# Eight units' products in plain float32, paired loads and two weight queues in an attention and MLP kernel

## The chip, the cores and the metric

The kernel runs on one core of one Trainium2 chip. A core has TensorE (PE, with its weight loads shown as PEld), VectorE (DVE), ScalarE (ACT), GpSimd (POOL) and SyncE (SP), and its DMAs share 16 DMA engines. The metric is the device time of the run in microseconds, lower is better.

## The reference

Attention with a window of 32 keys to either side and 32 global tokens, then an MLP on its output, all with float32 results. Eight batches, eight heads, 512 local and 32 global tokens, heads of 64:

```python
s_ll = np.where(np.abs(pos[:, None] - pos[None, :]) <= 32, scale * (q_l @ k_l.T), -1e9)
s_l = np.concatenate([scale * (q_l @ k_g.T), s_ll], axis=-1)
out_l = softmax(s_l) @ np.concatenate([v_g, v_l])          # local queries
out_g = softmax(scale * (q_g @ [k_g, k_l].T)) @ [v_g, v_l]  # global queries
x = concat([out_g, out_l]).transpose(0, 2, 1, 3).reshape(B * S, 512)   # 8 * 544 rows
h = x @ w_in                  # 512 x 2048
g = 0.5 * h * (1 + erf(h / sqrt(2)))
out = g @ w_out               # 2048 x 512
```

(shortened; the transposes of single heads are left out). The two weight matrices arrive as 64-bit floats, everything else as 32-bit.

## The kernel before, in words

**Units and keys.** Attention is cut into 64 *units*: batch, half of the local tokens (256 queries), pair of heads. The MLP is cut into 17 *keys*: one for each batch and half (256 rows, fed by four units) and one, "g", for the 256 rows of all global queries, which comes last. A key runs over 16 slices f of the 2048 hidden columns: `h` (12 matmuls of 128x256, L667 to L669), gelu on two slices at once (`gf`), its split (`gh`, `gl`) and `acc` (6 matmuls of 128x512, L696 to L698, three for each of two tiles of 128 rows). `ob` (L150) copies the two `acc` tiles out of PSUM, and SP stores them (L711, L715).

**Split products.** TensorE multiplies in a rounded form of float32 (fp32r in the rows). To keep float32 accuracy every operand is split: a copy in fp32r (high part) and the difference to it (low part, the subtractions of L157), and a product is the sum of three matmuls: high by high, low by high, high by low. So q becomes `q1` and `q2`, k `k1` and `k2`, v the tile `vs`, the transposed softmax `at`, the MLP's input `xh` and `xl`, and each weight `wi` and `wo` two halves of 512 columns.

**A unit.** SP loads k, q and v (`kn`, `qn`, `vr`; L330, L337, L281 to L292). For the first eight units (`NPE`) TensorE transposes k and q into PSUM (`kp` L344, `qp` L351); for later ones DVE does. Then come the splits; `s` (12 matmuls, L408: two windows, three terms, two heads); the masking with the maximum (L427); exp on ACT (L306); the normalisation (L457 to L461 on DVE, `ge` L468 and L473 on POOL or DVE); the transposes of the softmax (`t`, L482 to L485); `at` and its low part (L150, L496); `o` (8 matmuls, L512, whose output holds high and low terms side by side, 128 partitions by 256), which a copy on ACT (L517) and two additions on DVE (L522, L523) gather in `xs`; and `sg` (2 matmuls, L536), the scores of the global queries, which are collected in `sgr`. `xh` and `xl` are then made from `xs`.

**Weights.** 32 chunks of 512 KB, loaded by DMAs that ACT issues (`wraw`, L176 and L180), become float32 in five steps: `w1` (ACT L193), `w2` (ACT L197), `w3` (shift and or, DVE L201), `w4` (the high part, DVE or ACT, L152 or L150) and `w5` (the low part, L157 on POOL or DVE). The raw chunks live in two pools of three and four buffers; the memory of the pool of four is used by MLP tiles once its chunks are done.

**What sets the order.** A planner in Python (`step`, L721 on) builds a list of steps with the engine or engines that may run them, a modelled duration (`DUR`), what they need, which buffers they take and free, and a due time: the key's number times 60, less a lead for attention (`AHEAD`), plus a number for each kind of step (`OFF`, and `OFF0` too for the units and steps of the first two keys). It then plays the program: again and again it takes the step that could start first, and among those the one due first. The order that comes out is forced on each engine's queue, so an instruction that waits holds back all behind it on its engine. `EARLY` and `LATER` name the engines that may run a step.

Of the kernel before, what the change touches and what calls it, by code (L numbers as in the profile page):

```python
# [35 lines left out]
NB = 10  # L36
# [11 lines left out]
    "gmin": 0.8, "gex": 0.8, "gn": 0.55, "gt": 0.57, "gah": 0.5, "gal": 0.6, "gagh": 0.25, "gagl": 0.2,  # L48
# [9 lines left out]
AHEAD = 23.2  # L58
# [3 lines left out]
EARLY = {"gh": "a", "gl": "p", "gvc": "va", "gvl": "p", "k1": "va", "nf": "p", "ns": "pv", "q1": "va", "vc": "va", "vl": "p", "xh": "v", "xl": "vp"}  # L62
LATER = {"gh": "va", "gl": "p", "gvc": "va", "k1": "va", "ns": "p", "q1": "va", "vc": "va", "vl": "p", "w4": "va", "w5": "pv", "xh": "va", "xl": "vp"}

OFF = {
    "ah": -0.7, "al": 6.9, "b": -2.3, "c": -29.8, "e": -41.0, "g": -10.7, "gagh": 1.8,
    "gagl": -54.7, "gah": 6.3, "gal": -15.7, "gex": 14.0, "gh": 11.7, "gl": 9.5, "glv": 2.5,
    "gmin": -27.2, "gn": 11.1, "go": -11.0, "gsh": 1.1, "gsl": -36.6, "gt": 0.5, "gvc": -40.0,
# [3 lines left out]
    "sga": -6.9, "sgc": -6.1, "t": 0.4, "tg": 10.0, "tgh": -5.3, "tgl": -5.0, "tk": -0.4,  # L72
    "tq": 90.4, "vc": -12.0, "vl": -51.1, "vm": -24.8, "w1": 46.7, "w2": -27.2, "w3": -0.3,
    "w4": 1.1, "w5": 11.8, "wl": 5.5, "x": 14.9, "xh": -18.0, "xl": -0.4,
}
OFF0 = {
    "ah": -0.8, "al": -7.0, "b": -3.9, "c": -2.0, "e": 2.1, "g": -14.9, "gagh": -6.6, "gagl": -22.2,
    "gah": -2.9, "gal": -27.8, "gex": 11.7, "gh": 2.1, "gl": 2.6, "glv": -16.8, "gmin": -1.6,
    "gn": -44.0, "go": 9.5, "gsh": -16.7, "gsl": -15.1, "gt": 2.8, "gvc": 26.0, "gvl": -7.5,
# [6 lines left out]
}  # L86
NPE = 8
UNP = 100
WB = 10
# [3 lines left out]
def attn_mlp(ctx, tc, q_l, k_l, v_l, q_g, k_g, v_g, w_in, w_out, out):  # L93
# [178 lines left out]
    def load_v(e, u):  # L272
# [15 lines left out]
        for r0, src, s0, n in ef:  # L288
            nc.sync.dma_start(out=raw[r0:r0 + n, 4:6, :], in_=src[s0:s0 + n])
# [738 lines left out]
```

## Time and profile before

| | |
|---|---|
| median of 3 runs | 1084.24 us (1084.11 to 1084.83) |
| the profiled execution, its own time | 1083.86 us |
| its span in the trace | 1082.1 us |
| TensorE busy | 1026.0 us, 95% of the span, 7064 matmuls |
| DVE, ACT, POOL busy | 693.6, 695.1, 453.6 us |
| mean granted TensorE clock | 0.985 of full speed |
| loads and stores | 71.34 MB, 66 GB/s on average |
| chain that ended last | PE 89%, DMA 4%, DVE 4%, SP 1%, ACT 1% |

TensorE is the engine that is nearly always busy; the shares are means over the whole span, so a stage with another limit is hidden in them. Times of single instructions are in microseconds from the span's start. A busy time of an engine is the union of its instructions; neighbouring ones overlap a little, so the sum over groups of instructions is larger.

### The profile page before, as it was taken

To read this page: it belongs to the slowest core of one execution; us is meant where nothing else is said; L and a number is where in the kernel's file an instruction comes from. 1 tells how busy PE (TensorE), PEld (TensorE's weight loads), DVE (VectorE), ACT (ScalarE), POOL (GpSimd) and SP (SyncE) were. 2 spreads that over 40 slices of the span, in tenths; PEclk is the share of its full clock that TensorE was granted. 3 is DMA by queue.
4 is the path that set the end of the run, shared out by engine and by line. 5 is a ranking of instruction groups with operands and counts; after the bars stand their busy time and mean duration, and the time that the engine had idled before them with its cause. 6 is when DMAs were issued, how large, how long until landed. Compare 5 with 4: busy or idle time off the path is not lost.

```text
span 1082.1 us, 21840 instructions
## 1 busy us (share of the span) xinstructions
PE 1026.0 (95%) x7064; PEld 916.6 (85%) x7064; DVE 693.6 (64%) x2089; ACT 695.1 (64%) x1634; POOL 453.6 (42%) x548
## 2 busy tenths in 40 slices
PE   3759789999999999999999999999999999999997
PEld 2549578999999899998999988988899889999896
DVE  4777876768677776667666776667675776642000
ACT  4766766767686776657866676657864876663221
POOL 4444234534444454344434444334444544343121
PEclk9969979999999999999999999999999999999999
DMA  6455623323322322222322233222222223110000
GB/s 171 127 149 170 182 62 73 62 56 61 75 49 60 66 58 63 37 70 42 69 53 64 44 68 61 50 57 54 68 42 69 42 65 59 44 34 21 1 20 20
DMA packets 274738, 71.34 MB, mean 66 GB/s; under 512 B 260032, under 2 KB 268224, under 8 KB 274624
## 3 DMA queue, kind: packets, MB, share of 16 engines
q1 hardware_dynamic: 263872, 53.17, 23.4%
q10 hardware_dynamic: 10752, 16.78, 5.1%
q8 instruction: 56, 0.92, 0.4%
q14 instruction: 58, 0.48, 0.2%
HBM read 60.95 MB, written 8.91 MB: 65 GB/s over the span
## 4 chain that ended last, share of the span: by engine, by line
PE 89%; DMA 4%; DVE 4%; SPq 1%; ACT 1%; issue 1%; POOL 0%; ACTq 0%; DVEq 0%; POOLq 0%
PE h L667 12%; PE h L669 12%; PE h L668 12%; PE acc L696 11%; PE acc L698 11%; PE acc L697 11%; PE o L512 6%; PE s L408 5%; PE t L482 2%; PE go L622 2%; DMA kn<-in_k_l_dram 2%; PE sg L536 1%; PE t L483 1%; DMA vr<-in_v_l_dram 1%; PE gt L581 1%; DMA wraw<-in_moe_w_out_dram 1%
## 5 line engine op out<-in xcount | busy, mean ns | idle before, releaser
L667 PE MATMUL h<-xh,wi 128*128 128x256 f32 x1088 | 313.9, 289 | 11.3 <-POOL ge L468 6.1
L669 PE MATMUL h<-xh,wi 128*128 128x256 f32 x1088 | 305.8, 281 | 1.1 <-POOL wi L157 1.1
L668 PE MATMUL h<-xl,wi 128*128 128x256 f32 x1088 | 305.6, 281 | 0.1
L157 POOL TENSOR_TENSOR gl<-gf,gh 128x512 fp32r<-128x512 f32 x136 | 176.1, 1295 | 267.4 <-ACT gh L150 166.0
L667 PEld LDWEIGHTS h<-xh,wi 128*128 128x128 f32 x1088 | 206.4, 190 | 22.3 <-POOL ge L468 6.4
L696 PE MATMUL acc<-wo,gh 128*128 128x512 f32 x544 | 220.0, 404 | 1.7 <-DVE wo L152 1.7
L698 PE MATMUL acc<-wo,gh 128*128 128x512 f32 x544 | 215.1, 395 | 0.0
L697 PE MATMUL acc<-wo,gl 128*128 128x512 f32 x544 | 214.8, 395 | 0.0
L668 PEld LDWEIGHTS h<-xl,wi 128*128 128x128 f32 x1088 | 206.7, 190 | 6.6 <-DVE xl L157 0.4
L669 PEld LDWEIGHTS h<-xh,wi 128*128 128x128 f32 x1088 | 206.4, 190 | 1.3 <-POOL wi L157 1.3
L306 ACT ACTIVATE gf<-h 128x512 f32<-128x512 f32 x136 | 81.4, 598 | 103.0 <-PE h L669 88.8
L157 POOL TENSOR_TENSOR vs<-vr,vs 128x512 fp32r<-128x512 f32 x64 | 83.3, 1302 | 107.5 <-DVE vs L152 57.0
L698 PEld LDWEIGHTS acc<-wo,gh 128*128 128x128 f32 x544 | 102.0, 188 | 25.3 <-DVE wo L157 0.4
L306 ACT ACT_TABLE_LOAD x87 | 111.6, 1283 | 9.9 <-PE h L669 8.7
L696 PEld LDWEIGHTS acc<-wo,gh 128*128 128x128 f32 x544 | 102.2, 188 | 18.1 <-issue 1.9
L468 POOL TENSOR_TENSOR ge<-a_t,sm 128x256 f32<-128x256 f32 x64 | 60.2, 941 | 135.8 <-DVE sm L458 75.8
L306 ACT ACTIVATE a_t<-a_t,sm 128x192 f32<-128x192 f32 (+1 forms) x256 | 116.6, 457 | 0.5
L697 PEld LDWEIGHTS acc<-wo,gl 128*128 128x128 f32 x544 | 102.3, 188 | 13.5
L427 DVE CUSTOM_DVE_ANT_0 a_t<-s,mask 128x192 f32<-128x192 f32 (+1 forms) x256 | 80.9, 369 | 48.1 <-PE s L408 47.8
L496 DVE TENSOR_TENSOR at<-t,at 128x512 fp32r<-128x512 f32 (+1 forms) x128 | 75.6, 618 | 41.9 <-ACT at L150 41.4
L150 ACT ACTIVATE gh<-gf 128x512 fp32r<-128x512 f32 x98 | 61.8, 631 | 49.5 <-PE acc L698 48.4
L512 PE MATMUL o<-at,vs 128*128 128x256 f32 x512 | 80.1, 294 | 7.7 <-DVE at L496 7.7
(111 smaller groups left out, 1660.8 us busy)
## 6 DMA issues: line engine op xcount, KB each, us to landing
wraw<-in_moe_w_in_dram ACTq DMA_DIRECT2D x16, 512.0 KB, 4.3
wraw<-in_moe_w_out_dram ACTq DMA_DIRECT2D x16, 512.0 KB, 3.9
vr<-in_v_l_dram SPq DMA_DIRECT2D x128, 64.0 KB, 2.1
gvr<-in_v_l_dram SPq DMA_DIRECT2D x64, 128.0 KB, 2.5
out_dram<-ob SPq DMA_DIRECT2D x32, 256.0 KB, 2.1
kraw<-in_k_l_dram SPq DMA_DIRECT2D x224, 36.0 KB, 2.0
qraw<-in_q_l_dram SPq DMA_DIRECT2D x224, 32.0 KB, 1.9
vr<-in_v_l_dram SPq DMA_DIRECT2D x64, 32.0 KB, 2.2
```

The lines of the kernel that those rows point to most:

```text
L150: nc.scalar.activation(out=out, in_=in_, func=AF.Copy)
L157: (nc.vector if e == "v" else nc.gpsimd).tensor_sub(**kw)
L306: nc.scalar.activation(func=func, **kw)
L427: nc.vector.tensor_tensor_reduce(out=a_t[:, j, aoff[half][i]:aoff[half][i] + w], in0=s[:, c:c + w], in1=masks[half][:, c:c + w], scale=1.0 ...
L496: nc.vector.tensor_sub(out=at[:, 1], in0=st.pop((u, "t", j))[:, :n * P].rearrange("p (n q) -> p n q", q=P), in1=at.bitcast(F32)[:, 0])
L512: nc.tensor.matmul(out=o[:, :, qsl], lhsT=l.rearrange("p s e -> p (s e)"), rhs=r, start=(n == 0), stop=(n == 3), skip_group_check=True)
L667: nc.tensor.matmul(out=h, lhsT=hi, rhs=xh, start=(c == 0), stop=False, skip_group_check=True)
L668: nc.tensor.matmul(out=h, lhsT=hi, rhs=xl, start=False, stop=False, skip_group_check=True)
L669: nc.tensor.matmul(out=h, lhsT=lo, rhs=xh, start=False, stop=(c == NCC - 1), skip_group_check=True)
L696: nc.tensor.matmul(out=acc[t], lhsT=gh[:, f % 2, tsl], rhs=hi, start=(f == 0), stop=False)
L697: nc.tensor.matmul(out=acc[t], lhsT=gl[:, f % 2, tsl], rhs=hi, start=False, stop=False)
L698: nc.tensor.matmul(out=acc[t], lhsT=gh[:, f % 2, tsl], rhs=lo, start=False, stop=(f == NF - 1))
```

## The change

The first eight units (keys (0, 0) and (0, 1)) multiply in plain float32, with no low parts: `st_k0` and `st_q0` copy k and q out of PSUM, `s` is 4 matmuls instead of 12 and `sg` 1 instead of 2, `st_a0` copies the transposed softmax once, `st_o0` makes 8 matmuls of 64x128 out of v as it was loaded, and `st_c0` copies the result to `xs` in two instructions. Their k, q and v are loaded for two units at once into tiles (`raws`, `vr`) that are set up once; k of the global tokens isn't loaded a second time for batch 0. Loads of weights may be issued by SP as well as ACT (`WLE`), as the planner finds. The first four slices of `h` of key (0, 0) go to the PSUM banks of `acc` and one quarter after the other, as their part of `xh` is there (`HQ`). For the last two slices of key "g" the twelve `acc` matmuls are ordered by tile, `ob` of the second tile may run on either engine, its last `gl` runs on DVE, and ACT issues two of the eight stores. Nearly all numbers of `OFF`, `OFF0`, some of `DUR` and the engines in `EARLY` and `LATER` are new; `ALAP` and `DELTA` are switched off.

```diff
-AHEAD = 23.2
+AHEAD = 7.41
...
-    "ah": -0.7, "al": 6.9, "b": -2.3, "c": -29.8, "e": -41.0, "g": -10.7, "gagh": 1.8,
+    "ah": 3.1, "al": -21.0, "b": -70.1, "c": -34.1, "e": -32.8, "g": -12.4, "gagh": 7.5,
...
+WLE = "as"
...
+HQ = 4
 NPE = 8
 UNP = 100
-WB = 10
+WB = 14
...
-            nc.scalar.dma_start(
+            (nc.sync if e == "s" else nc.scalar).dma_start(
...
-    def load_v(e, u):
+    def load_v(e, u, n=1):
...
+        raw = vr[:, :, i0:i0 + n].rearrange("p s i j e -> p s (i j) e")
+        vh, gh = v_l[b, 2 * p:2 * p + 2 * n].rearrange("h s e -> s h e"), v_g[b, 2 * p:2 * p + 2 * n].rearrange("h s e -> s h e")
...
+        kl, kg = k_l[b, 2 * p:2 * p + 4].rearrange("h s e -> s h e"), k_g[b, 2 * p:2 * p + 4].rearrange("h s e -> s h e")
...
+    def st_q0(e, u):
+        t = ap_.tile([P, CH], F32, name="qt", tag="qt")
+        copy(e, t, st[u, "qt"])
+        st[u, "qt"] = t
...
+        prods = [(st[u, "qt"], st[u, "kt"])] if (u, "kt") in st else [(q1, k1), (q2, k1), (q1, k2)]
         for i, (k0, w, qt) in enumerate(windows(half)):
-            for n, (qq, kk) in enumerate(((q1, k1), (q2, k1), (q1, k2))):
+            for n, (qq, kk) in enumerate(prods):
...
+    def st_a0(e, u, j):
+        n = 4 if j == 0 else 3
+        at = ap_.tile([P, n, P], F32, name=f"ao{j}", tag=f"at{j}")
+        st[u, "at", j] = at
+        copy(e, at, st.pop((u, "t", j))[:, :n * P].rearrange("p (n q) -> p n q", q=P))
...
+    def st_o0(e, u):
...
+        for n, (slot, qsl) in enumerate(((ts_, qs), (tf, qf), (2, qf), (3, qs))):
+            for j in range(2):
+                a = at0 if n == 3 else (at0, at1)[j]
+                nc.tensor.matmul(out=o[0:64, j, qsl], lhsT=vr[:, slot, u[2] % 2, j, :], rhs=a[:, n, :],
+                                 start=(n == 0 and j == 0), stop=(n == 3), skip_group_check=True)
+
+    def st_c0(e, u):
+        o = st.pop((u, "o", 0))
+        for j in range(2):
+            copy(e, xs[64 * j:64 * j + 64, u[2]], o[0:64, j])
...
+            if key == (0, 0) and f < HQ:
+
+                st["h", key, f // 2] = ps_o.tile([P, 2, CH], F32, name="h", tag=f"acc{f // 2}")
...
-        for t in range(2):
+
+        last = key == "g" and f >= NF - 2
+        for t, f in ([(f - NF + 2, x) for x in (NF - 2, NF - 1)] if last else [(t, f) for t in range(2)]):
...
-                nc.sync.dma_start(out=out[r0:r0 + SG, :], in_=o[32 * n:32 * n + 32, :])
+                (nc.sync if t == 0 or n % 2 == 0 else nc.scalar).dma_start(out=out[r0:r0 + SG, :], in_=o[32 * n:32 * n + 32])
...
-            step(("gl", key, f), ml_gl, (key, f), "p", d + 1.3, [("gh", key, f)], [("gl", (key, f))], [("gf", (key, f))], early=not n)
+            step(("gl", key, f), ml_gl, (key, f), "v" if key == "g" and f == NF // 2 - 1 else "p", d + 1.3, [("gh", key, f)], [("gl", (key, f))], [("gf", (key, f))], early=not n)
```

On TensorE, what stands right before the first h product of the program is, in the kernel before, `s` of a unit with its three terms and `sg` with two (`k_141` and `q_143` are the high parts, `k_142` and `q_144` the low ones):

```order
L408 MATMUL s<-k_141,q_143 128x192 x2
L408 MATMUL s<-k_141,q_144 128x192 x2
L408 MATMUL s<-k_142,q_143 128x192 x2
L408 MATMUL s<-k_141,q_143 128x224 x2
L408 MATMUL s<-k_141,q_144 128x224 x2
L408 MATMUL s<-k_142,q_143 128x224 x2
L536 MATMUL sg<-k_141,gs 128x256
L536 MATMUL sg<-k_142,gs 128x256
L667 MATMUL h<-xh,wi 128x256
```

and in the changed kernel, at the same place:

```order
L439 MATMUL s<-kt,qt 128x192 x2
L439 MATMUL s<-kt,qt 128x224 x2
L369 MATMUL qp<-ident,raws 128x128 x2
L361 MATMUL kp<-ident,raws 128x128 x2
L363 MATMUL kp<-ident,raws 128x64
L592 MATMUL sg<-kt,gs 128x256
L726 MATMUL h<-xh,wi 128x256
```

`s` went from 12 to 4 matmuls and `sg` from 2 to 1, and the transposes of the next unit's q and k (`qp`, `kp`) moved in between.

On SP, the loads of k and v of one of the first eight units are, in the kernel before:

```order
L330 DMA kn<-in_k_l_dram 128x2x64
L330 DMA kn<-in_k_l_dram 32x2x64
L330 DMA kn<-in_k_g_dram 32x2x64
L330 DMA kn<-in_k_l_dram 64x2x64 x2
L281 DMA vr<-in_v_l_dram 128x2x64 x2
L289 DMA vr<-in_v_l_dram 32x2x64
L289 DMA vr<-in_v_g_dram 32x2x64
L289 DMA vr<-in_v_l_dram 64x2x64
L292 DMA vr<-in_v_g_dram 32x64 x2
L292 DMA vr<-in_v_l_dram 32x64 x2
```

and in the changed one, where a load brings two units and loads of weights stand between them:

```order
L354 DMA raws<-in_q_l_dram 128x4x64 x2
L186 DMA wraw<-in_moe_w_out_dram 128x1024
L345 DMA raws<-in_k_l_dram 128x4x64
L345 DMA raws<-in_k_l_dram 32x4x64
L345 DMA raws<-in_k_g_dram 32x4x64
L345 DMA raws<-in_k_l_dram 64x4x64
L348 DMA raws<-in_k_l_dram 64x2x64 x2
L182 DMA wraw<-in_moe_w_in_dram 128x4x256
L295 DMA vr<-in_v_l_dram 128x4x64 x2
L303 DMA vr<-in_v_l_dram 32x4x64
L303 DMA vr<-in_v_g_dram 32x4x64
L303 DMA vr<-in_v_l_dram 64x4x64
```

Each load has four heads where it had two, and the weights' loads moved from ACT's queue in between them.

On TensorE, at the end of the program, the last h product of key "g" and what follows it, in the kernel before (36 `acc` matmuls follow in all, to the end in this alternation of the two tiles):

```order
L669 MATMUL h<-xh,wi 128x256
L696 MATMUL acc_14031<-wo,gh 128x512
L697 MATMUL acc_14031<-wo,gl 128x512
L698 MATMUL acc_14031<-wo,gh 128x512
L696 MATMUL acc_14032<-wo,gh 128x512
L697 MATMUL acc_14032<-wo,gl 128x512
L698 MATMUL acc_14032<-wo,gh 128x512
```

and in the changed kernel (12 follow in all; the five left out here are of the second tile):

```order
L728 MATMUL h<-xh,wi 128x256
L757 MATMUL acc_13548<-wo,gh 128x512
L758 MATMUL acc_13548<-wo,gl 128x512
L759 MATMUL acc_13548<-wo,gh 128x512
L757 MATMUL acc_13548<-wo,gh 128x512
L758 MATMUL acc_13548<-wo,gl 128x512
L759 MATMUL acc_13548<-wo,gh 128x512
L757 MATMUL acc_13549<-wo,gh 128x512
```

The last h moved 24 matmuls towards the end, and the tiles no longer alternate.

## Rows read from the trace of the kernel before

**Rows 1.** Busy time by stretch: window, length, busy of five engines, PEclk, DMA share, GB/s.
```profile
0.00:77.20 77.20, 40.94 (x181) 29.41 (x181) 51.36 (x152) 47.62 (x114) 35.85 (x64) 0.91 0.58 155
77.20:150.50 73.30, 60.95 (x386) 52.97 (x386) 61.13 (x152) 55.03 (x117) 26.12 (x29) 0.92 0.52 145
...
500.00:600.00 100.00, 99.61 (x714) 89.77 (x712) 68.71 (x214) 67.11 (x160) 43.41 (x55) 1.00 0.28 59
10.00:20.00 10.00, 6.08 (x30) 4.20 (x31) 6.37 (x22) 5.42 (x16) 1.59 (x3) 1.00 0.68 192
110.00:120.00 10.00, 8.24 (x56) 6.83 (x54) 7.98 (x21) 6.58 (x12) 2.60 (x2) 1.00 0.75 219
```

**Rows 2.** Timeline of PE: start, us, instruction; in brackets idle before and releaser.
```profile
77.19 0.55 PE L667 MATMUL h<-xh,wi 128*128 128x256 f32 x1 [6.14 <-POOL ge L468]
...
150.47 0.58 PE L667 MATMUL h<-xh,wi 128*128 128x256 f32 x1 [3.89 <-DVE xh L152]
```

**Rows 3.** Chain of waits from 0 to 78 us: shares by line, then pieces (start, us).
```profile
by line: DMA kn<-in_k_l_dram 22.0%; DMA vr<-in_v_l_dram 11.6%; DMA wraw<-in_moe_w_out_dram 9.9%; SPq L330 9.1%; DMA qn<-in_q_l_dram 5.8%; issue 4.5%; PE o L512 4.0%; SPq L281 3.6%; DMA vr<-in_v_g_dram 3.4%; PE kp L344 3.0%; PE s L408 1.9%; 
...
1.75 5.37 DMA kn<-in_k_l_dram
...
31.64 0.43 PE t L482 x2
```

**Rows 4.** Chain of waits around 300 us: pieces on PE (start, us).
```profile
297.77 0.22 PE t L482 x2
...
298.53 0.12 PE h L667
...
299.94 0.86 PE s L408 x12
300.80 1.15 PE o L512 x8
301.95 0.23 PE acc L696
...
303.35 0.26 PE sg L536 x2
```

**Rows 5.** DVE by line and shape, 77.2 to 150.5 us: busy, mean ns, idle before.
```profile
L157 DVE TENSOR_TENSOR wo<-wraw,wo 128x512 fp32r<-128x512 f32 x7 | 4.8, 687 | 0.1
...
L522 DVE TENSOR_TENSOR xs<-o,xs 64x256 f32<-64x256 f32 x8 | 3.3, 414 | 0.5 <-ACT xs L517 0.3
```

**Rows 6.** DVE by line, 0 to 77.2 us.
```profile
L201 DVE SCALAR_TENSOR_TENSOR wraw<-wraw 128x512 int32<-128x512 int32 x12 | 8.4, 702 | 7.9 <-ACT wraw L197 7.9
L427 DVE CUSTOM_DVE_ANT_0 a_t<-s,mask 128x192 f32<-128x192 f32 (+1 forms) x24 | 7.6, 369 | 0.2 <-PE s L408 0.2
L496 DVE TENSOR_TENSOR at<-t,at 128x512 fp32r<-128x512 f32 (+1 forms) x8 | 4.9, 622 | 2.5 <-ACT at L150 2.4
L461 DVE TENSOR_TENSOR a_t<-a_t,sm 128x512 f32<-128x512 f32 x5 | 4.4, 870 | 0.2
...
L152 DVE CAST wi<-wraw 128x512 fp32r<-128x512 f32 x3 | 1.3, 423 | 0.1
...
L559 DVE TENSOR_SCALAR gsm<-gsm 128x1 f32<-128x1 f32 x1 | 0.2, 153 | 0.0
```

**Rows 7.** DMA issues: count, KB each, median us from issue to landing.
```profile
wraw<-in_moe_w_in_dram ACTq DMA_DIRECT2D x16, 512.0 KB, 4.3
...
out_dram<-ob SPq DMA_DIRECT2D x8, 64.0 KB, 1.7
```

**Rows 8.** Timeline of the end, ACT and SP.
```profile
1067.81 0.60 ACT L306 ACTIVATE gf<-h 128x512 f32<-128x512 f32 x1 [2.19 <-PE h L669]
1070.61 0.63 ACT L150 ACTIVATE gh<-gf 128x512 fp32r<-128x512 f32 x1 [2.20 <-PE acc L698]
...
1075.45 1.30 ACT L150 ACTIVATE ob<-acc 128x512 f32<-128x512 f32 x2 [4.21 <-PE acc L698]
...
1076.07 3.63 SPq L711 DMA_DIRECT2D out_dram<-ob  x8
```

More of the change, by code (lines that the diff above doesn't have):

```diff
@@ L666, in ml_hc @@
         hi, lo = wi[:, f, c * P:c * P + P], wi[:, f, 512 + c * P:512 + c * P + P]
-        nc.tensor.matmul(out=h, lhsT=hi, rhs=xh, start=(c == 0), stop=False, skip_group_check=True)
+        nc.tensor.matmul(out=h, lhsT=hi, rhs=xh, start=(c == 0 and not (key == (0, 0) and f < HQ and f % 2)), stop=False, skip_group_check=True)
         nc.tensor.matmul(out=h, lhsT=hi, rhs=xl, start=False, stop=False, skip_group_check=True)
@@ L798, in attn_mlp @@
         g = (b, p // 2) if half else None
-        bx = [("b", x) for x in both] + ([("gmin", g)] if g else [])
+        bx = [("b", x) for x in both] + ([("gmin", g)] if g and GX else [])
         for j in range(2):
@@ L810, in attn_mlp @@
-        step(("al", u, 1), st_al, (u, 1), "v", f0 - 3.4, [("ah", u, 1)], [], [("t", (u, 1))], dur="al1")
-        step(("lv", u), load_v, (u,), "s", f0 - 18.0, [("o", units[n - 2], 1)] if n > 1 else [], [("vr", u)], issues=9, size=0.25, after=pu and ("lv", pu))
-        step(("vm", u), st_vm, (u,), "p", f0 - 8.0, [("lv", u)])
-        step(("vc", u), st_vc, (u,), "va", f0 - 6.0, [("vm", u)], [("vs", u)], early=n < 8)
-        step(("vl", u), st_vl, (u,), "p", f0 - 4.5, [("vc", u)], [], [("vr", u)], early=n < 8)
@@ new lines, in attn_mlp @@
+        if n < NPE and not odd:
+            step(("lv", u), load_v, (u, 2), "s", f0 - 18.0, [], [("vr0", u), ("vr1", units[n + 1])], issues=9, size=0.5, after=("lv", units[n - 2]) if n else None)
+            step(("vm", u), st_vm, (u, 2), "p", f0 - 8.0, [("lv", u)])
+        elif n >= NPE:
+            step(("lv", u), load_v, (u,), "s", f0 - 18.0, [("o", units[n - 2], 1)], [("vr%d" % odd, u)], issues=9, size=0.25, after=("lv", pu if n > NPE else units[n - 2]))
+            step(("vm", u), st_vm, (u,), "p", f0 - 8.0, [("lv", u)])
@@ L855, in attn_mlp @@
             w = [("w5", 2 * f)] if not n else []
-            if f in (0, NF - 1):
+            if not n and f < HQ:
+                for c in range(NCC):
+                    step(("hc", key, f, c), ml_hc, (key, f, c), "t", C0 + W * f + 0.1 * c,
+                         w + [("hc", key, f, c - 1) if c else ("hc", key, f - 1, 0) if f else None, ("xl", key, c)],
+                         [("acc", "h")] if not f and not c else [], [("xx%d" % c, key)])
+            elif f in (0, NF - 1):
                 for c in range(NCC):
@@ L862, in attn_mlp @@
             else:
-                step(("h", key, f), ml_h, (key, f), "t", C0 + W * f, w + [("h", key, f - 1) if f > 1 else ("hc", key, 0, NCC - 1)],
+                step(("h", key, f), ml_h, (key, f), "t", C0 + W * f,
+                     w + ([("hc", key, x, NCC - 1) for x in range(HQ)] if not n and f == HQ else [("h", key, f - 1) if f > 1 else ("hc", key, 0, NCC - 1)]),
                      hb, [("xx%d" % c, key) for c in range(NCC)])
@@ L869, in attn_mlp @@
             d = C0 + W * (2 * f + 2)
-            step(("g", key, f), ml_g, (key, f), "a", d, [("h", key, 2 * f + 1) if 2 * f + 1 < NF - 1 else ("hc", key, NF - 1, NCC - 1)], [("gf", (key, f))], [("h", (key, f))], table="gelu")
+            step(("g", key, f), ml_g, (key, f), "a", d, [("hc", key, x, NCC - 1) for x in (2 * f, 2 * f + 1)] if not n and 2 * f < HQ else [("h", key, 2 * f + 1) if 2 * f + 1 < NF - 1 else ("hc", key, NF - 1, NCC - 1)], [("gf", (key, f))], [("h", (key, f)) if n or 2 * f >= HQ else ("acc", "h")], table="gelu")
@@ new lines, in attn_mlp @@
+    if ALAP:
+        todo, after = {}, {}
+        for x in nodes.values():
+            todo[x["name"]] = 0
+        for x in nodes.values():
+            for y in x["needs"]:
+                todo[y] += 1
+        stack = [x for x in nodes.values() if not todo[x["name"]]]
+        while stack:
+            x = stack.pop()
+            nm = x["name"]
+            kind = nm[0]
+            if nm in after and kind not in ("h", "hc", "mo") and not (kind[0] == "g" and kind not in ("g", "gh", "gl")):
+                x["due"] = after[nm] - min(x["eng"].values()) + OFF.get(kind, 0.0)
+            for y in x["needs"]:
+                after[y] = min(after.get(y, 1e9), x["due"] - 0.3)
+                todo[y] -= 1
+                if not todo[y]:
+                    stack.append(nodes[y])
@@ L940, in attn_mlp @@
                         due += 100.0
-                c = (t, due, ENG.index(k), x, k)
-                if best is None or c[:3] < best[:3]:
-                    best = c
-        assert best, "no step can start"
+                can.append((t, due, ENG.index(k), x, k))
+        assert can, "no step can start"
+        first = min(can, key=lambda c: c[:3])
+        best = min((c for c in can if c[4] == first[4] and c[0] <= first[0] + DELTA.get(first[4], 0.0)), key=lambda c: (c[1], c[0]))
         t, due, _, x, k = best
```

220 lines of the change are left out of this document (129 added, 91 removed), and 27 rows, old and new, of tables (DUR, OFF, OFF0).

## The prediction

> **What bounds the kernel now.** I read the busy time by stage first, then the chain of waits of the start, then single instructions. The stages [rows 1] show a TensorE that is full from some 160 us on (99.61 of 100 us busy in the stretch from 500 us) and whose unit and MLP work there is not touched by the change. What can move lies at the two ends. Up to 77.2 us TensorE is busy 40.9 us, in short pieces; there the first four units go through attention and no product of the MLP runs. At 77.19 us the first h product starts, after 6.14 us of idle [rows 2]. From there to 150.5 us it is busy 61.0 of 73.3 us. At 150.47 us the last quarter of the second key's first h product starts, after 3.89 us of idle behind an xh [rows 2]; from then on there is always work. I call 0 to 77.2 us stage one, 77.2 to 150.5 us stage two and their end the handover.
>
> In the instruction order of the changed kernel the handover is the same place: the products of units 0 to 7 are done, 201 of the h matmuls stand before it in both, and 72 of acc where it was 78. What follows it is the same work to within those 6 matmuls (1.4 us). So the time is: the profiled 1083.86 us, less what the handover moves forward, and what the tail changes. The profiled execution is 0.4 us under the median of the runs.
>
> The chain of waits of stage one [rows 3] names the reason for its length: loads of k 22.0%, of v 11.6% and 3.4%, of q 5.8% and of weights 9.9% are 52.7% of 78 us, 41 us of landing time, in ten pieces one behind the other, the first of 5.4 us, and SP's own issuing is 12.7% more (10 us). Neither DVE (51.4 of 77.2 us) nor ACT (47.6) is full [rows 1].
>
> **The change part by part.** *Loads by pairs.* Of units 0 to 7 two share one set of loads: some 17 DMAs in place of 31, with the same bytes. On the chain I count six landings where ten stood (k of pairs 0, 1 and 2, v of pairs 0 and 1, one weight), and half of SP's issuing: 41 x 4/10 + 5 = 21 us less, the first h at 56 us. What is late next is DVE or the bytes. DVE: counted along the changed order up to the last xl before the first h, at the means of [rows 5, 6]: 14 shift-ors at 0.70 us, 10 casts at 0.42 and 7 subtractions at 0.69 of weights, 22 score reductions at 0.37, four normalisations of 0.87, ten copies out of PSUM at the cast's 0.42, and some 10 us of smaller ones: 44 us. Neighbours overlap: the 27 groups of stage one before add to 57 us, of which [rows 6] shows the largest and the last, where the union is 51.4, so 44 becomes 40 us. At DVE's present share (51.4 of 77.2) that is 60 us. Bytes: up to the first h the kernel moves 155 GB/s x 77.2 us = 12.0 MB [rows 1], and the changed one wants the same by its own first h (16 weight loads of 0.52 MB each, four pairs of k and q, two to three of v). At the 192 GB/s that the stretch from 10 to 20 us reached [rows 1] these are 62.5 us, at the 219 of the stretch from 110 us 55, at today's mean 77. I take the first h at 63 us, since the bytes are the latest of the three; ends 55 and 77.
>
> *Weights on two queues.* Each of 32 loads may now be issued from SP or ACT; SP takes 26 of them in the order. A load of w_in lands 4.3 us after its issue [rows 7] and would from either, so the gain is only that ACT's instructions no longer stand behind an issue that waits for a buffer. I price that at nothing (below nothing is the second rival). The Trainium skill, "DMA: Bandwidth & Descriptors", section "Issuing engines are not separate DMA queues", says that DMAs from different engines run on the same 16 DMA engines, and that a second issuing engine saves only sequencer time. By that the second queue brings no bytes per second, which is the first rival; the price of nothing agrees with it.
>
> *Plain float32 products, units 0 to 7.* DVE and POOL lose the low halves. Stage two on DVE, from [rows 5] and their like: sixteen xs additions (8 of them 3.3 us, their twins as much) become four copies, 5.0 less; eight low halves of at (4.9 us, as in stage one [rows 6]) become five copies of 0.6 like ACT's [rows 8], 1.9 less; nine casts and low halves of k, q and vs at some 0.42 [rows 6], 3.8 less; against that 18 weight subtractions in place of 13 (POOL gives them up), 3.4 more, two casts (0.8), normalisations, reductions and ge that the planner puts there, 2.0 more. 61.1 becomes 56.6 us, which at the present share of 83% is 68 us. TensorE pays: in a full stretch s of a unit takes 0.86, o 1.15 and sg 0.26 us [rows 4]. No plain float32 product is in the trace. The nearest rows are float32 transposes: two of 128 columns in 0.22 us at full clock, in 0.43 us at the start [rows 3], so 0.11 to 0.21 us per 128 columns. For s (4 of 208 columns), sg (288) and o (8 of 128) that is 1.8 to 3.7 us a unit, against 2.3 now: from 0.4 less to 1.4 more. I take 1.4, since a product of two full operands is hardly cheaper than moving one. Units 0 to 3 lie in stage one, where TensorE idles 36 us. Units 4 to 7 cost 5.6 us in stage two, whose 12.4 us of idle cover it; TensorE needs 61 + 5.6 = 66.6 us there, and 5.6 us would be the price if the cover were gone. The Trainium skill, "FP8 and Floating Point Precision", section "TensorE Precision Notes", gives true float32 four passes. At four times the 0.12 us of a split product of 256 columns [rows 4] that is an estimate of 4.0 us a unit, 1.7 more than today, 6.8 us in stage two, still under its idle time.
>
> So stage two wants 68 us of DVE at its share and 66.6 of TensorE, in place of 73.3. Two engines that full wait for each other; I take 71, ends 64 and 78. The handover is at 63 + 71 = 134 in place of 150.5: 16.5 us earlier.
>
> *The tail.* Today both acc tiles end within 0.7 us, ACT copies both in 1.30 us and SP issues eight stores in 3.63 us, the last landing 1.7 us after its issue [rows 7, 8]. The last twelve products are now ordered by tile, so the first tile ends six products of 0.23 us [rows 4], 1.4 us, before the last one, 0.7 earlier than now, and its four stores go out beside the second tile's products. ACT takes two stores of the second tile. The last issue starts some 1.6 us earlier; nothing hides that. But the order also moves the last h. Before, 36 products of acc follow it (8.4 us), and the first 24 cover the last gelu, gh and gl. Now twelve follow, all of them of that last pair, so TensorE waits: gelu 0.60 and gh 0.63 [rows 8], gl now on DVE 0.69 [rows 5], four handovers of 0.1 (gelu starts 0.1 after the last h [rows 8]), 2.3 us, of which one product that needs gh alone fills 0.2. That is 2.0 us of idle that is not there today. The tail is 0.4 us longer; ends 1.6 less, if the wait is hidden after all, and 1.0 more.
>
> *The planner.* All due times, the lead of attention over the MLP (23.2 to 7.41) and some durations are new, so every key after the handover has a new order with the same work. At [rows 1]'s 0.39 us of idle per 100 us there is nothing to win. I price it at nothing; it can only lose (third rival).
>
> Sum: 1083.86 - 16.5 + 0.4 = 1067.8, with the 0.4 to the median 1068 us.
>
> **The rivals.** First, the bytes: loads stay at 155 GB/s as in stage one now, the first h stays at 77, stage two takes 71, handover 148: 1083.86 - 2.3 + 0.4, or 1082 us. For it: the same bytes, on the same 16 engines. Against: the DMA share there is 0.58, and 0.75 at 219 GB/s [rows 1].
>
> Second, slower: unit loads stuck behind weights on SP. In the new order loads of q, k (twice) and v stand behind weight loads that must wait until an older chunk's buffer is converted: load 4.3 [rows 7], ACT 2 x 0.6 as its copies take [rows 8], DVE 0.70 + 0.42 [rows 6] and 0.69 [rows 5], some 7 us a turn. At four places before the first h that is up to 28 us: 1096 us. It turns the result from 4 us a place on (16.1 us over four). Against: the buffers are seven there, and in today's start SP waits little for weights. The opposite, that these waits replace waits of ACT, is in my sum.
>
> Third, the new order stalls after the handover: one more DVE step of 0.7 us [rows 5] ahead of the first h at each of 15 key changes is 10.5 us, 1078 us. For it: attention runs 16 us closer to its use, and in the order the h of a new key is cut into quarters between o's. Against: nothing but TensorE is full there.
>
> That the change doesn't do what it says I leave out: the built order has four s matmuls where twelve stood, and the paired loads.
>
> **How the numbers follow.** Forecast, 1058 to 1075 us: 0.61. Still earlier handover (55 + 64 = 119, 31.5 earlier): 0.07, down to 1053. First rival 0.12, third 0.09, second 0.11. The range from 1056 to 1081 holds the forecast, half of the early case, most of the third rival and of the first what comes out a little under its 1082. 0.2% is 2.2 us, about what a measurement can tell from no change, so same is 1082.1 to 1086.4. Faster 0.82 (forecast, early case, third, half of the first), same 0.07 (the rest of the first, a little of the second), slower 0.11.
>
> **What would show it.** The first h near 63 us and the handover near 134. The chain up to there with k and v landings in about six pieces; DMA near 190 GB/s in stage one; DVE about 40 and 57 us busy in the two stages. Plain s and o at about 0.2 us per 128 columns. If the first h comes at 75 or later with DMA under 165 GB/s, the first rival holds; if SP waits for w5 of a chunk ahead of a unit's loads and TensorE for those, the second; if TensorE idles over 5 us after 160 us, the third. The tail: 2 us of idle on TensorE behind the last h, and from the last product to the end 1.6 us less.

## The result, and the profile after

The changed kernel takes 1068.62 us (median of 4 runs, 1066.75 to 1069.45) where the kernel before takes 1084.53: a ratio of 0.9851, with a 95% interval of 0.9834 to 0.9868. The prediction was 1068 us. The total came out, but two of its steps did not, and they cancel: that it came so close is luck.

The profiled execution took 1066.75 us, its span is 1064.9 us. The marks that cut the span into stages, with the prediction and with a second profiled execution (1068.59 us):

| us | before | predicted | after | after, again |
|---|---|---|---|---|
| first h | 77.2 | 63 | 56.9 | 57.3 |
| handover (last quarter of the second key's first h) | 150.5 | 134 | 125.9 | 129.5 |
| from there to the end of the last product | 925.6 | 927.6 | 933.0 | 932.4 |
| from there to the end of the span | 6.0 | 4.4 | 6.0 | 4.9 |

The handover comes 24.5 us earlier (21.0 in the second execution) where 16.5 were forecast; of these, 7.4 (6.8) are given back between the handover and the last product, where 2.0 were forecast.

Busy time by stretch of the changed kernel (window, length, busy of PE, PEld, DVE, ACT, POOL, PEclk, DMA share, GB/s); the first two stretches answer to the first two of [rows 1], and the third is the rest up to the last product:

```profile
0.00:56.90 56.90, 37.35 (x188) 25.10 (x189) 38.62 (x118) 40.02 (x98) 18.41 (x40) 0.97 0.75 215
56.90:125.90 69.00, 61.62 (x421) 53.66 (x420) 61.99 (x152) 52.89 (x119) 15.64 (x17) 1.00 0.53 146
125.90:1058.90 933.00, 925.82 (x6489) 831.69 (x6487) 547.36 (x1764) 603.77 (x1432) 380.88 (x434) 1.00 0.25 52
20.00:30.00 10.00, 9.57 (x36) 6.73 (x37) 6.85 (x23) 9.47 (x28) 5.40 (x6) 1.00 1.05 343
```

The kernel before from its handover to its last product, and stage two in the second execution of the changed kernel:

```profile
150.50:1076.10 925.60, 924.08 (x6499) 834.26 (x6499) 581.08 (x1788) 591.80 (x1404) 391.60 (x456) 1.00 0.25 52
```

```profile
57.30:129.50 72.20, 66.23 (x421) 58.01 (x420) 63.25 (x154) 52.75 (x119) 15.86 (x18) 0.92 0.53 140
```

To be seen there: stage one moves 215 GB/s where it moved 155, and 343 in its best ten microseconds. DVE is busy 38.6 of 56.9 us (40 were forecast), then 62.0 of 69.0 (56.6 were forecast). TensorE idles 7.4 us in stage two instead of 12.4. In this execution the granted clock of stage two is 1.00 where it was 0.92; in the second one it is 0.92 again, and the stage is 3.2 us longer though TensorE idles 1.4 us less of it. From the handover to the last product TensorE idles 7.2 us where it idled 1.5.

The chain of waits of the new stage one, by line (its answer to [rows 3]; the row is cut off at its end):

```profile
by line: DMA raws<-in_k_l_dram 12.0%; ACT a_t L322 9.6%; DMA wraw<-in_moe_w_in_dram 8.9%; ACT wraw L199 6.6%; DMA wraw<-in_moe_w_out_dram 6.5%; issue 6.1%; PE o L562 5.8%; ACT wraw L203 4.6%; DVE wraw L207 3.5%; SPq L306 3.3%; PE sg L592 3.
```

Loads of k are 12.0% where they were 22.0, and no load of v is in the part shown, nor of q; ACT's exponentials and weight conversions have moved up.

Timeline of TensorE: the marks, the plain `o` of a unit at full clock (the trace has two records for each plain float32 product, so x16 is eight products), the two longest idles after the handover, and the end (start, us, instruction; in brackets idle before and releaser):

```profile
56.95 0.47 PE L726 MATMUL h<-xh,wi 128*128 128x256 f32 x1
...
66.65 1.96 PE L562 MATMUL o<-ao,vr 128*64 128x128 f32 x16 [1.42 <-DVE ao L158]
...
125.93 0.28 PE L726 MATMUL h<-xh,wi 128*128 128x256 f32 x1
...
192.79 0.50 PE L592 MATMUL sg<-k,gs 128*128 128x256 f32 x2 [1.05 <-DVE sm L458]
202.29 0.41 PE L513 MATMUL t<-ident,a_t 128*128 128x128 f32 x2 [1.85 <-DVE a_t L492]
...
1053.60 0.28 PE L728 MATMUL h<-xh,wi 128*128 128x256 f32 x1
1055.29 0.50 PE L757 MATMUL acc<-wo,gh 128*128 128x512 f32 x1 [1.41 <-ACT gh L156]
1056.08 0.50 PE L758 MATMUL acc<-wo,gl 128*128 128x512 f32 x1 [0.28 <-DVE gl L163]
```

And what issues the last stores there:

```profile
1058.17 4.34 SPq L772 DMA_DIRECT2D out_dram<-vr  x6
1059.58 1.34 ACTq L772 DMA_DIRECT2D out_dram<-vr  x2
```

Six issues take 4.34 us, 0.72 each with what lies between them, where eight took 3.63 [rows 8], 0.45 each.

### The profile page after: what moved, and what is told of

Same layout as the page of the kernel before. It is cut to its first block, busy times and chain, and to the rows that moved or that the text cites. A ratio compares the mean times of both kernels' runs of the same rounds, so it can differ in the third digit from the quotient of the medians.

```text
span 1064.9 us, 21622 instructions
## 1 busy us (share of the span) xinstructions
PE 1024.8 (96%) x7096; PEld 910.4 (85%) x7096; DVE 648.0 (61%) x2032; ACT 697.3 (65%) x1648; POOL 414.9 (39%) x491
## 4 chain that ended last, share of the span: by engine, by line
PE 85%; ACT 4%; DVE 4%; DMA 3%; SPq 1%; issue 1%; POOL 0%; ACTq 0%; DVEq 0%; POOLq 0%
PE h L726 11%; PE acc L757 11%; PE acc L758 11%; PE acc L759 11%; PE h L728 11%; PE h L727 11%; PE o L549 5%; PE s L439 4%; PE t L513 2%; DMA wraw<-in_moe_w_in_dram 2%; PE go L677 2%; PE sg L592 1%; PE t L514 1%; ACT L322 1%; DMA raws<-in_k_l_dram 1%
## 5 line engine op out<-in xcount | busy, mean ns | idle before, releaser
L322 ACT ACTIVATE gf<-h 128x512 f32<-128x512 f32 x136 | 81.1, 596 | 76.2 <-PE h L728 56.9
L163 POOL TENSOR_TENSOR vs<-vr,vs 128x512 fp32r<-128x512 f32 x56 | 72.9, 1302 | 146.8 <-ACT vs L156 36.9
L533 DVE TENSOR_TENSOR at<-t,at 128x512 fp32r<-128x512 f32 x112 | 68.3, 621 | 35.3 <-ACT at L156 34.3
L156 ACT ACTIVATE gh<-gf 128x512 fp32r<-128x512 f32 x103 | 65.0, 631 | 36.1 <-PE acc L759 34.3
L156 ACT ACTIVATE at<-t 128x512 fp32r<-128x512 f32 x112 | 59.2, 546 | 36.6 <-PE t L516 19.7
L577 DVE TENSOR_TENSOR xs<-o,xs 64x256 f32<-64x256 f32 x112 | 46.6, 416 | 58.1 <-ACT xs L572 54.3
```

The source lines that it names most:

```text
L156: nc.scalar.activation(out=out, in_=in_, func=AF.Copy)
L163: (nc.vector if e == "v" else nc.gpsimd).tensor_sub(**kw)
L322: nc.scalar.activation(func=func, **kw)
L533: nc.vector.tensor_sub(out=at[:, 1], in0=st.pop((u, "t", j))[:, :n * P].rearrange("p (n q) -> p n q", q=P), in1=at.bitcast(F32)[:, 0])
```

## The experiments

Times are medians; ratios are to the kernel before on the same chip, with 95% intervals. The mark for all is the changed kernel run again.

**The changed kernel again.**

> The changed kernel once more, as the mark for the next three on the same chip. Expected 1068.6 us again (0.985 of before), with the handover near 126 us and 2.1 us of waits of TensorE behind the last h.

Measured: 1068.62 us, ratio 0.9848 (0.9834 to 0.9861). The waits behind the last h are there; the handover came at 129.5 us. So the start scatters by some 3 us from execution to execution, and a single profile's handover says no more than that. Nearly all of the 3.6 us lies in stage two, where the granted clock was 0.92 and not 1.00. The first h scatters less: in this kernel and the three below that leave its start as it is (the last h earlier, the last stores, the k load ahead), it comes at 56.9 to 58.7 us.

### What makes the start shorter

**Single loads.**

> The changed kernel with each paired load of k, q and v cut into two loads of one unit each, one after the other at the same place, same bytes. Theory (the pairs save landings and issues, 5 of 21 us by issues alone): the first h comes about 5 us later than 57, the run 3 to 6 us longer than the changed kernel. Rival (bytes alone count): within 1 us of it.

```diff
-            nc.sync.dma_start(out=kn[r0:r0 + n, 4 * t:4 * t + 4], in_=src[s0:s0 + n])
+            for i in range(2):
+                nc.sync.dma_start(out=kn[r0:r0 + n, 4 * t + 2 * i:4 * t + 2 * i + 2], in_=src[s0:s0 + n, 2 * i:2 * i + 2])
```

(Cut: q and v in the same way.) Measured: 1085.13 us, ratio 1.0002 (0.999 to 1.0015). The whole gain is gone, far more than either theory gave. The first h is at 70.9 us and the handover at 143.7. What TensorE waited for in stage one (us in total, times, longest):

```profile
PE qp L375 <- DMA raws<-in_q_l_dram: 13.4, 5, 7.6
PE kp L367 <- DMA raws<-in_k_l_dram: 7.7, 2, 4.0
```

In the changed kernel these two are 2.0 and 3.6 us over the whole run. Counting the issues of SP in the trace up to the first h: 124 before (59.5 us of issuing in 77.2), 75 in the changed kernel (37.8 in 56.9), 114 here (55.5 in 70.9). An issue takes 0.48 to 0.50 us on average in all three; for a load of q the median is 0.44 us with 128 KB in the changed kernel and 0.45 with 64 KB here. So SP, which the chain of [rows 3] shows with 12.7%, was busy issuing for 77% of stage one before. What of the time up to the first h SP spent not issuing is 17.7, 19.1 and 15.4 us in the three, so the first h moved with the issue time. The load behind TensorE's longest wait here, the second pair's q, on SP in the changed kernel, then on SP and TensorE here (start, us):

```profile
15.42 0.98 SPq L354 DMA_DIRECT2D raws<-in_q_l_dram  x2
```

```profile
21.74 1.97 SPq L360 DMA_DIRECT2D raws<-in_q_l_dram  x4
...
26.87 0.79 PE L375 MATMUL qp<-ident,raws 128*128 128x128 f32 x2 [7.62 <-DMA raws<-in_q_l_dram]
```

It stands at the same place in the program and is issued 6.3 us later, with SP issuing without a pause worth the name from 7.6 to 23.7 us.

**Single loads, half of them issued by GpSimd.**

> The changed kernel with the paired loads cut in two as before, but the second unit's half issued by GpSimd instead of SP. Single loads on SP alone put the first h at 70.9 us, with 114 issues on SP before it where the changed kernel has 75. Theory (SP's issue time of about 0.48 us each is what the pairs save): back to a first h of 57 to 61 us and 1069 to 1073 us. Rival (the number of transfers and their landings counts, whoever issues them): first h near 70 us, 1083 us.

Against the run above (cut: q, v and the last pieces of k in the same way):

```diff
-                nc.sync.dma_start(out=kn[r0:r0 + n, 4 * t + 2 * i:4 * t + 2 * i + 2], in_=src[s0:s0 + n, 2 * i:2 * i + 2])
+                (nc.gpsimd if i else nc.sync).dma_start(out=kn[r0:r0 + n, 4 * t + 2 * i:4 * t + 2 * i + 2], in_=src[s0:s0 + n, 2 * i:2 * i + 2])
```

Measured: 1069.79 us, ratio 0.9845 (0.9825 to 0.9866), the changed kernel's within the intervals; first h at 60.3 us with 77 issues on SP (35.3 us) and 53 on GpSimd (32.6 us) ahead of it. The transfers are as many and as small as in the run above, and only the queue that issues half of them differs. DMA issues up to 60.3 us (count, KB, us to landing):

```profile
raws<-in_q_l_dram SPq DMA_DIRECT2D x8, 64.0 KB, 4.3
raws<-in_q_l_dram POOLq DMA_DIRECT2D x8, 64.0 KB, 3.9
vr<-in_v_l_dram SPq DMA_DIRECT2D x6, 64.0 KB, 3.4
vr<-in_v_l_dram POOLq DMA_DIRECT2D x6, 64.0 KB, 2.4
raws<-in_k_l_dram SPq DMA_DIRECT2D x4, 64.0 KB, 5.3
raws<-in_k_l_dram POOLq DMA_DIRECT2D x4, 64.0 KB, 3.4
```

The theory holds: what the pairs save is in the main SP's time to issue, not landings and not bytes; 2 to 3 us of the first h stay.

**All weights on ACT's queue.**

> The changed kernel with all loads of weights issued by ACT, each at the place in the program where it stands now. Theory (price nothing): the first h and the handover stay within 1.5 us, since the same 16 engines carry the bytes: 1068 to 1070 us. Rival: the second queue is what shortens the start, since ACT's steps stand behind issues that wait for a buffer: first h and handover 3 to 10 us later, 1072 to 1079 us.

```diff
-            (nc.sync if e == "s" else nc.scalar).dma_start(
+            nc.scalar.dma_start(
```

(Cut: the other line that loads weights in the same way.) Measured: 1072.96 us, ratio 0.9888 (0.9869 to 0.9906). The second queue is worth some 4 us, as the rival has it, though the first h (59.7) moved less than it said and the handover (131.4) is within the scatter of one profile. SP issues 60 DMAs before the first h here and has time to spare; the weights stand on ACT, with its exponentials and conversions, which the chain of the changed kernel shows to be late next. I call the sign shown, and the mechanism only argued.

**The low parts made again, and not used.**

> The changed kernel with the low parts of q, k and the transposed softmax of the first eight units made on DVE again and not used; TensorE's products stay plain. This adds about 2.15 us of DVE a unit, 17 us in all. Theory (DVE is late next in both stages): most of it shows, 8 to 15 us longer than the changed kernel. Rival (bytes and landings decide): under 4 us.

```diff
         copy(e, t, st[u, "qt"])
+        nc.vector.tensor_sub(out=q2, in0=st[u, "qt"], in1=t)
```

(Cut: k and the transposed softmax in the same way.) Measured: 1082.22 us, ratio 0.9974 (0.9964 to 0.9984), 13.6 us more than the changed kernel: the theory's 8 to 15. The first h is at 66.3 us, the handover at 139.6. The groups that were put back, DVE up to 66.3 us (busy, mean ns, idle before):

```profile
L532 DVE TENSOR_TENSOR ao<-t,ao 128x512 f32<-128x512 f32 (+1 forms) x8 | 5.0, 624 | 1.5 <-ACT ao L156 1.3
...
L381 DVE TENSOR_TENSOR q<-qp,qt 128x256 fp32r<-128x256 f32 x7 | 2.9, 421 | 1.3 <-ACT qt L156 1.2
L387 DVE TENSOR_TENSOR k<-kp,kt 128x320 fp32r<-128x320 f32 x6 | 2.9, 486 | 3.3 <-ACT kt L156 3.3
```

10.8 us of DVE before the first h made it 9 us later. With the pairs kept, DVE's low parts alone take back 13.6 of the 16 us; with plain products kept, single loads take back all of it. The two gains do not add: SP's issuing and DVE stood one close behind the other, and each edit is worth its time only beside the other.

**The o products twice.**

> The changed kernel with the o products of the first eight units made twice with the same result: about 2 us more of TensorE a unit, 16 us in all. Theory (TensorE's idle time covers it in stage one, and nearly in stage two): 2 to 6 us longer than the changed kernel. Rival (TensorE or the chain through o decides): 10 to 16 us longer.

```diff
-        for n, (slot, qsl) in enumerate(((ts_, qs), (tf, qf), (2, qf), (3, qs))):
+        for n, (slot, qsl) in [x for _ in range(2) for x in enumerate(((ts_, qs), (tf, qf), (2, qf), (3, qs)))]:
```

Measured: 1072.93 us, ratio 0.9881 (0.9857 to 0.9906), 4.3 us more, for 16 us (eight units at 1.96) of added products: nearly three quarters are hidden, as the theory says.

**The old tables.**

> The changed kernel's edits planned with the due times, lead, engine choices and early weight buffers of the kernel before (the durations stay the new ones). The prediction priced the new tables at nothing. Theory (edits by themselves bring it): first h under 62 us and a run within 5 us of the changed kernel. Rival (the gain is in the order, which was made for the other loads): first h over 65 us and 1076 us or more.

```diff
-AHEAD = 7.41
+AHEAD = 23.2
-WB = 14
+WB = 10
```

(with `OFF`, `OFF0`, `EARLY` and `LATER` of the kernel before.) Measured: 1210.32 us, ratio 1.1144 (1.1128 to 1.1161). Both were half right. The first h comes at 57.7 us and the handover at 138.9, so the shorter stage one does not need the new tables; but from the handover to the last product it takes 1064.4 us in place of 933.0. TensorE idles 99.0 us of that where it idled 7.2, and is busy 965.3 us where it was busy 925.8, at a mean granted clock of 0.96 in place of 1.00. What TensorE waited for most:

```profile
PE go L677 <- POOL vgs L163: 23.2, 6, 3.9
PE gx L693 <- DVE gsm L625: 21.0, 6, 4.0
PE o L549 <- DVE at L533: 18.0, 20, 1.6
```

These are steps of attention after the start that the change does not touch. The new tables place them so that they are hidden; the old ones, with the new buffers, steps and durations, do not. Which of the tables matters was not tried.

Not tried alone: the early weight buffers, which went with the tables, the k of the global tokens that isn't loaded twice, and the four slices of h in quarters. The first slice was in quarters before, too, so the mark of the first h owes nothing to the last of these.

### What is lost after the handover

**The last h earlier.**

> The changed kernel with the last h product of key g put 24 acc products earlier, as far from the end as before; all else in the planned order. My theory: TensorE's wait for the last gelu, gh and gl (1.57 and 0.55 us after the last h in the trace of the changed kernel) goes and nothing takes its place: 2.0 us less than the changed kernel. Rival: the wait only moves, because the stores or POOL's gl end last: within 0.5 us of it.

```diff
+    moved = [('hc', 'g', 15, 0), ('hc', 'g', 15, 1), ('hc', 'g', 15, 2), ('hc', 'g', 15, 3)]
+    held = {e[2]["name"]: e for e in order if e[2]["name"] in moved}
+    order = [e for e in order if e[2]["name"] not in moved]
+    at = [e[2]["name"] for e in order].index(('mo', 'g', 10))
+    order[at:at] = [held[n] for n in moved]
```

Measured: 1066.12 us (1065.66 to 1066.31), ratio 0.9823 (0.9809 to 0.9836): 2.5 us less than the mark. From the handover to the last product it takes 930.5 us in place of 933.0 and 932.4. The wait was a loss and nothing took its place.

The wait can cost more than its own length. In the second execution of the changed kernel the granted clock is 0.50, the lower of its two levels, from 1058.6 us on, and the last products follow each other at 0.43 us in place of 0.23. The last products, first in that execution, then in the first one:

```profile
1059.62 0.63 PE L758 MATMUL acc<-wo,gl 128*128 128x512 f32 x1
1060.05 0.63 PE L759 MATMUL acc<-wo,gh 128*128 128x512 f32 x1
```

```profile
1057.58 0.39 PE L758 MATMUL acc<-wo,gl 128*128 128x512 f32 x1
1057.82 0.39 PE L759 MATMUL acc<-wo,gh 128*128 128x512 f32 x1
```

From the start of the last h to the start of the last product that makes 6.2 us in place of 4.9. Of the ten traces with twelve products behind the last h, six have it (6.0 to 6.5 us); of the four with 36 behind it, none (8.3 us in all four).

**The last stores from contiguous tiles.**

> The changed kernel with the output tiles of key g (ob) in contiguous memory instead of four strided pieces of 512 bytes per partition. My theory: the strided pieces make an issue of a store 0.6 to 0.7 us long where it was 0.42, and took away the 1.6 us that the prediction gave to the stores; so issues fall to about 0.42, the time from the last product to the end from 6.0 to about 4.4, and the run is 1.6 us shorter. Rival: two queues issuing at once are what makes an issue long; then issues stay at 0.6 and the time within 0.5 us.

```diff
+        if key == "g":
+            st[key, "ob", t] = o = raws[:, 640 * t:640 * t + 512]
+            copy(e, o, acc)
+            return
```

Measured: 1067.07 us, ratio 0.9828 (0.9815 to 0.9842), 1.6 us less than the mark; the intervals overlap, so the verdict rests on the traces. From the end of the last product to the end it takes 4.1 us in place of 6.0 and 4.9. In this execution, as in the one with 4.9, the last products ran at the lower clock, and the first tile's stores had more time beside them: 0.8 us less, like with like. At the full clock to the last product stand the run with the last h earlier, 6.0 us with strided tiles, and the run of all edits below, 4.5 with contiguous ones: 1.6 us. The issues:

```profile
1059.28 3.34 SPq L776 DMA_DIRECT2D out_dram<-raws  x6
1061.85 0.85 ACTq L776 DMA_DIRECT2D out_dram<-raws  x2
```

ACT's two take 0.42 us each instead of 0.67; of SP's six the single instructions in the trace last 0.32 to 0.57, where they lasted 0.57 to 0.73. The packets of the end (eight stores and one packet on the instruction queue), first in the changed kernel, then here:

```profile
DMA packets 1153, 0.53 MB, mean 59 GB/s; under 512 B 128, under 2 KB 1152, under 8 KB 1152
```

```profile
DMA packets 385, 0.53 MB, mean 53 GB/s; under 512 B 128, under 2 KB 128, under 8 KB 384
```

The change had put `ob` into the tile `vr`, where a row of 512 numbers lies in four pieces. The same bytes left in three times the packets, and each issue took longer. Two queues at once are not the reason: both issue here, too.

**The tail's order in the kernel before.**

> The kernel before with only the last twelve acc products ordered by tile and two of the second tile's stores issued by ACT; its output tiles are contiguous there. The prediction gave this edit 1.6 us. Theory: it does so where issues take 0.42 us: the time from the last product to the end falls from 6.0 to about 4.4 us, the run is 1.6 us shorter (ratio 0.9985). Rival (the last landing or the closing sequence sets the end): no change.

```diff
-        for t in range(2):
+        last = key == "g" and f >= NF - 2
+        for t, f in ([(f - NF + 2, x) for x in (NF - 2, NF - 1)] if last else [(t, f) for t in range(2)]):
```

(Cut: ACT issues two of the second tile's stores.) Measured: 1082.67 us, ratio 0.9974 (0.9965 to 0.9984), 2.7 us less than before by the medians; in the trace the end after the last product falls from 6.0 to 4.3 us, the 1.6 us that were expected (5.96 and 4.34); the other 1.1 us are not placed. SP's six issues take 2.69 us:

```profile
1075.69 2.69 SPq L713 DMA_DIRECT2D out_dram<-ob  x6
1077.09 0.84 ACTq L713 DMA_DIRECT2D out_dram<-ob  x2
```

**The k load ahead of the v loads.**

> The changed kernel with the k load of unit (1,1,3) issued on SP ahead of the v loads of unit (1,1,1), which wait for a buffer. My theory: TensorE's stall of 2.0 us at 200 us, where the transposes of that k on DVE hold back a softmax, goes: 2 us less than the changed kernel. Rival: DVE is late there anyway and the stall stays or moves to the v: within 0.5 us of it, or slower.

```diff
+    moved = [('lk', (1, 1, 3))]
+    at = [e[2]["name"] for e in order].index(('lv', (1, 1, 1)))
```

(moved as the last h was.) Measured: 1066.49 us, ratio 0.983 (0.9816 to 0.9844), 2.1 us less than the mark by the medians, with intervals that overlap. The trace does not bear that out in full:

```profile
203.47 0.41 PE L513 MATMUL t<-ident,a_t 128*128 128x128 f32 x2 [0.17 <-DVE a_t L492]
206.69 0.39 PE L726 MATMUL h<-xh,wi 128*128 128x256 f32 x1 [1.25 <-ACT gf L322]
```

The idle of 1.85 us before that transpose is down to 0.17, so the late k load was its cause; but TensorE then waits 1.25 us for a gelu that it did not wait for. Some 0.4 us remain for sure. The rest hangs on the clock. In the first execution of the changed kernel the granted clock is 0.50 from 204.1 to 207.4 us, behind the idle of 1.85, and h products follow at 0.21 us in place of 0.12:

```profile
204.58 0.41 PE L727 MATMUL h<-xl,wi 128*128 128x256 f32 x1
204.79 0.41 PE L728 MATMUL h<-xh,wi 128*128 128x256 f32 x1
...
207.67 0.28 PE L727 MATMUL h<-xl,wi 128*128 128x256 f32 x1
207.79 0.28 PE L728 MATMUL h<-xh,wi 128*128 128x256 f32 x1
```

In its second execution, with 1.50 us of idle there, and in this run the clock stays at 1.00. From the handover to the start of the last h the three take 927.7, 925.7 and 925.3 us.

**The three together, and one step more.**

> The changed kernel with three edits together: the last h of key g 24 products earlier, key g's output tiles contiguous, and the k load of unit (1,1,3) ahead of the v loads of unit (1,1,1). Theory (three separate losses): 2.5 + 1.6 + 2.1 us less than the changed kernel, about 1062.5 us. Rival (the second and third gain were scatter of the runs): 1065 to 1066 us.

The kernel that ran has a fourth edit, which the expectation doesn't name: where the `sg` of a unit stands right behind its `s`, the product of the MLP that follows is put ahead of `sg`.

```diff
+    for u in units:
...
+        order.remove(y)
+        order.insert(g, y)
```

By the order in the traces it moved one `sg`, the one behind 1.06 us of idle in the run above (195.38 us); there TensorE now idles 0.28 and 0.42 us, so some 0.4 us of what follows are its own.

Measured: 1064.15 us (1060.64 to 1067.37), ratio 0.9799 (0.9778 to 0.9819), the fastest version of this study, 4.5 us under the changed kernel where 6.2 were expected of three edits. That lies between the theory and the rival. From the handover to the end of the span its profile has 933.9 us (929.4 to the last product and 4.5 behind it) against 939.0 and 937.3: 3.4 to 5.1 less. Its profile is that of the slowest of its runs, with the handover at 131.7 us; where the others gain is not shown.

## Why the prediction was right, step by step

**What bounds the kernel** held: most of what moved lies before the handover or in the tail, and TensorE is nearly full between (7.2 us of idle in 933.0). One sentence did not: I wrote that 72 acc products stand before the handover in the new order; it is 84, against 78. That is 1.4 us of work the other way.

**Loads by pairs**: the first h was forecast at 63 us and came at 56.9, within the ends of 55 and 77. The mechanism was half right. I counted landings on the chain (41 us x 4/10) and gave SP's issuing 5 us. The two runs with single loads show that issuing was nearly all of it: 39 issues put back on SP alone cost 14.0 us of first h (70.9), put back half on GpSimd 3.4 (60.3), with as many landings. The chain of waits charges a load to "DMA" from its issue to its landing, and doesn't say that it was issued late because SP was at the issue before. The sum of SP's issues up to the first h, 59.5 of 77.2 us, would have hinted at it. Nor is it SP alone: the low parts made again put the first h at 66.3 us with 78 issues on SP.

The **bytes**, which set my 63, were mis-sized: 192 GB/s is no ceiling, since the changed kernel moved 215 on average in stage one and 343 for ten microseconds. The first rival falls with that.

**Two queues for the weights**: priced at nothing, worth some 4 us. The Trainium skill, "DMA: Bandwidth & Descriptors", section "Issuing engines are not separate DMA queues", adds that the sequencer time saved is usually small beside the transfer. In this case it was not small: 0.48 us an issue, 124 times before the first h. By which way the second queue for the weights gains its 4 us is only argued.

**Plain products** held in size: in the changed kernel, s takes 0.95 us, o 1.96 and sg 0.70, 3.6 us a unit (the first two units' s, at 14.8 and 20.9 us, take 1.86 and 1.76 at a granted clock of 1.00, and no row says why); 3.7 was taken (its own rows give 3.6), and the products made twice show that such a cost is mostly hidden. On DVE the prediction counted stage one without the low parts, but set the first h by the bytes; made again, the low parts cost 9.4 us of the first h, so DVE and not the bytes stood next. Of the Trainium skill's four passes ("FP8 and Floating Point Precision", section "TensorE Precision Notes") the estimate was 4.0. For o the trace agrees: eight products of 128 columns in 1.96 us are 0.245 each, four times the 0.06 that 128 columns of a split product take [rows 4]; s came out cheaper (four products of 208 columns in 0.95 us), sg no cheaper (0.70 us for 256 columns). The chain's rows for s and sg:

```profile
56.60 0.70 PE sg L592 x2
...
64.33 0.95 PE s L439 x8
```

**Stage two** was forecast at 71 us and took 69.0 (72.2 in the second execution, at a granted clock of 0.92). DVE has 62.0 us there and not 56.6, but at 90% of the stretch and not 83%: the term was too small and its share too low.

**The tail**: the wait behind the last h was forecast at 2.0 us. By the starts of the products shown above (1053.60, 1055.29 and 1056.08, where the next would have followed after 0.12 and 0.23) it is 2.1 us (2.3 less 0.2, as the prediction should have had it); moving the h back gained 2.5. That step was right, but it left out what the wait can do to the clock. The gain of 1.6 us at the stores did not come (6.0 us before and after), because I had not seen that the store's source was now strided. Without that, it is there: 1.6 us in both kernels.

**The planner** was priced at nothing after the handover, with a rival of 10.5 us. It cost some 5 us more than the tail explains (7.4 - 2.0). TensorE's idles of 0.74, 1.05 and 1.85 us between 184 and 203 us, where attention's new order meets the first units with split products, are 3.6 of it. The third rival's direction was right, its place (each change of key) was not: most of the loss sits at one place. The rest is not idle time but busy time: TensorE is busy 925.8 us from the handover on where it was 924.1, with 1.4 us less of acc to do. The products at half clock behind the idle of 1.85 us are some 1.5 us of that; the kernel before had its own such stretch behind its handover (granted clock 0.57 from 148 to 156 us), so the two busy times can't be set against each other to the microsecond, and what is left stays open.

So the forecast of 1068 is right by a handover 8.0 us better than forecast and a remainder 7 us worse (4.5 and 5.3 in the second execution). The direction and the two edits that bring it, paired loads and no low parts, were right; that the total came so close is luck.

## What to carry to other kernels

Add up the issue time of each queue for a stage before you trust the chain of waits there: a load that "takes" 4 us may have been late because its queue was busy issuing others. Before you call the sum a bound, move half of the issues to another queue. When two engines are nearly equally late, price edits together and not one by one. When a tile moves into another tile's memory, look at what its stores and loads become: the order of the instructions doesn't show it, the shape of the transfer does.

## What the runs showed of the hardware

- Issuing a DMA took SP 0.48 to 0.52 us on average before the first h, and a load of q 0.44 us in the median with 128 KB, 0.45 with 64 KB; GpSimd took 0.62 (32.6 us for 53). A queue can be late with its transfers far from any limit (DMA share 0.58 in [rows 1]).
- Eight stores whose source rows lie in four pieces of 512 bytes leave in 1153 packets instead of 385, one on the instruction queue counted in both, and an issue takes SP 0.57 to 0.73 us there, where the last eight of the kernel before take 0.45 with what lies between them.
- Ten microseconds at 343 GB/s, with a DMA share of 1.05, were reached in stage one (338 and 1.03 in the second execution); before, the stretch from 110 us had 219 [rows 1].
- The granted clock of stage two was 1.00 in one execution of the changed kernel and 0.92 in the other, as in the kernel before [rows 1]. Behind an idle of 1.4 and 0.3 us at the end it fell to its lower level, 0.50, in six of ten traces, and the last products then took 1.1 to 1.5 us longer.
- A plain float32 product of 128 columns takes 0.245 us at full clock (o); the trace has two records for it.
